# Down projection of row-tile pairs by one-level Strassen, with operand sums in float32r

## The chip, the cores and the metric

The kernel runs on one core of one Trainium2 chip. The metric is the device time of one execution in microseconds (us). "Before" is an already tuned kernel; "the changed kernel" is the same kernel with the change. PE is the matrix engine TensorE (PEld its weight loads), DVE is VectorE, ACT is ScalarE, POOL is GpSimd. PSUM is the memory with eight banks that PE accumulates in, SBUF the working memory.

## The reference, cut to what matters

Part A is a spectral filter with modulation. It is not touched. Part B is a gated feed-forward layer on 2048 rows of 640 values, with 1728 hidden columns, and its result is scaled by `gb` and added to the residual:

```python
def _B_ref(x, w_gate, w_up, w_down):
    g = _silu(x @ w_gate)          # 2048x640 @ 640x1728
    u = x @ w_up
    return g * u @ w_down          # 2048x1728 @ 1728x640
...
h = _layernorm(x, axis=-1) * (1 + cb) + sb
x = x + gb * _B_ref(h, B_w_gate, B_w_up, B_w_down)
```

## The kernel before

The 16 row tiles of 128 rows go through part B in five chunks of 2, 4, 4, 4 and 2 tiles. A chunk first makes the activations `AT` (13 full blocks of 128 hidden columns and one half block, number 13), then does the down projection of its tiles.

```python
chunks = [(0, 2), (2, 4), (6, 4), (10, 4), (14, 2)]
for ci, (t0, n) in enumerate(chunks):
    ...
    AT = (rE if ci % 2 == 0 else rX).cut(0, [NFC, N])
    gu13 = next_banks()[:, 0, 0:N]                       # the half block, gate and up together
    for c5 in range(NC5):
        nc.tensor.matmul(gu13, lhsT=Wp13[:, c5, :], rhs=h2T[:, :, c5, :], ...)      # L822
    ...
    for fc in range(NFC - 1):
        gu = next_banks()
        ...                                              # 5 gate matmuls L836, 5 up matmuls L839
        nc.scalar.activation(sg[:], gu[:, 0, 0:N], ACT.Silu)                        # L842
        nc.vector.tensor_tensor(AT[:, fc, :], gu[:, 1, 0:N], sg[:], ALU.mult)       # L843
        ...
        if ci == 0:      # chunk 0 also scales the down weights by gb, on VectorE
            for f2 in ((13, 0), (1, 2))[fc] if fc < 2 else (fc + 1,) if fc < 12 else ():
                nc.vector.tensor_tensor(Wd_sb[:, f2, :], Wd_sb[:, f2, :], gb_bc[:], ALU.mult)   # L848
            ...          # and normalises chunk 1: ln2_xn is L749, ln2_mod is L764
    for tl in range(n):
        t = t0 + tl
        if tl % 2 == 0:
            pops = [next_banks() for _ in range(2)]
            for h in range(2):
                for s in range(2):                       # half block: 64 rows of the array
                    rows = slice(64 * s, 64 * s + 64)
                    nc.tensor.matmul(pops[s][:, h, 0:320], lhsT=AT[rows, 13, 64 * tl:64 * tl + 128],
                                     rhs=Wd_sb[rows, 13, 320 * h:320 * h + 320], start=True, stop=False)   # L882
        ops4 = pops[tl % 2]
        for lo, hi in ((0, 320), (320, 640)):
            op = ops4[:, lo // 320, 0:320]
            for fc in range(NFC - 1):
                nc.tensor.matmul(op, lhsT=AT[:, fc, tl * 128:(tl + 1) * 128], rhs=Wd_sb[:, fc, lo:hi],
                                 start=False, stop=(fc == NFC - 2))                 # L888
        ...                                              # add the residual x1, store
```

A pair of tiles thus takes 2 x 2 x 13 = 52 full matmuls of 320 columns, and four on half of the array's rows.

Of the kernel before, what the change touches and what calls it, by code (L numbers as in the profile page):

```python
# [9 lines left out]

F32 = mybir.dt.float32
BF16 = mybir.dt.bfloat16
I32 = mybir.dt.int32
ACT = mybir.ActivationFunctionType
ALU = mybir.AluOpType

S, D, FF = 2048, 640, 1728
NT, P = 16, 128
# [3 lines left out]
NFC = 14  # L22
# [106 lines left out]
class _Region:  # L129


    def __init__(self, pool, name, nbytes):
        self.t = pool.tile([P, nbytes // 2], BF16, name=name)

    def cut(self, off, shape, dt=BF16, parts=P):
        n = int(np.prod(shape))
        el = 4 if dt == F32 else 2
        ap = self.t[0:parts, off // 2:off // 2 + n * el // 2]
        if dt == F32:
            ap = ap.bitcast(F32)  # L140
        if len(shape) > 1:
            names = " ".join(f"a{i}" for i in range(len(shape)))
            ap = ap.rearrange(f"p ({names}) -> p {names}", **{f"a{i}": v for i, v in enumerate(shape)})
        return ap
# [8 lines left out]
def adaln_block_kernel(ctx, tc, A_x, A_w_r, A_w_i, B_x, B_w_gate, B_w_up, B_w_down, c, w_mod, out):  # L153
    nc = tc.nc
# [8 lines left out]
    out_v = out.rearrange("o (p t) d -> p (o t) d", t=NT)  # L163
# [2 lines left out]
    const = ctx.enter_context(tc.tile_pool(name="const", bufs=1))  # L166
    big = ctx.enter_context(tc.tile_pool(name="big", bufs=1))

    rX = _Region(big, "rX", 20480)
    rM = _Region(big, "rM", 40960)  # L170
    rA = _Region(big, "rA", 20736)
    rE = _Region(big, "rE", 40960)
    rW = _Region(big, "rW", 49152)
    rH = _Region(big, "rH", 8192 + 2560)
    rL = _Region(big, "rL", 15360 + 4608)


    Ktab = const.tile([P, 576], BF16, name="Ktab")
# [36 lines left out]
    o = 0  # L215
# [6 lines left out]
    oGS = o; o += 768 * 4  # L222
    oSQ = o; o += 256

    SL = rL.cut(15360, [5, 2, 128])

    psum = ctx.enter_context(tc.tile_pool(name="psum", bufs=1, space=bass.MemoryType.PSUM)).tile([P, 8, 512], F32, name="psum")

    def banks(b, n, shape=None, dt=F32):
        ap = psum[:, b:b + n, :].rearrange("p b e -> p (b e)")  # L230
        if dt == BF16:
            ap = ap.bitcast(BF16)
        if shape is not None:
            ap = ap[:, 0:int(np.prod(shape))]
            if len(shape) > 1:
                ap = ap.rearrange("p (a b) -> p a b", a=shape[0])
        return ap
# [87 lines left out]
    if True:  # L325
# [86 lines left out]
        for k in range(NC5):  # L412
# [5 lines left out]
                                op=ALU.add)  # L418
# [73 lines left out]
    if True:  # L492
# [18 lines left out]
        Wd_sb = rA.cut(0, [NFC, D])  # L511
# [65 lines left out]
        def stage_b(g, PP):  # L577
            n = len(groups[g])
            yps = banks(g % 2, 1, [4, 128])
            for ps in (1, 0):  # L580
                for i in range(n):
                    nc.tensor.matmul(yps[:, i, :], lhsT=_rev(PP, 128 * n * ps + i, [[n, 128]]), rhs=identb[:],  # L582
                                     start=(ps == 1 and i == 0), stop=(ps == 0 and i == n - 1))
            Y2 = rL.cut(12288 + 1024 * (g % 4), [4, 128])
            nc.scalar.copy(Y2[:, 0:n, :], yps[:, 0:n, :])  # L585
            return Y2

# [155 lines left out]
    def ln2_pow(t0, n):  # L743
        v = rstd2[:, t0:t0 + n]
        nc.gpsimd.tensor_tensor(v, v, mhalf[:, 0:n], ALU.pow)  # L745
# [5 lines left out]
    def ln2_tr(ci):  # L751
        n = chunks[ci][1]
        nc.sync.dma_start_transpose(
            h2T_all[:, ci % 2, 0:n].rearrange("p tl c q -> p (tl c) q"),
            xn2c[:, 0:n].rearrange("p tl (c q) -> p (tl c) q", c=NC5))
# [48 lines left out]
                ln2_mod(0)  # L804


    oF = 14336
    pair = [1]

    def next_banks():  # L810
        b = banks(2 * pair[0], 2, [2, 512])
        pair[0] = (pair[0] + 1) % 4
        return b

    for ci, (t0, n) in enumerate(chunks):
        N = 128 * n
        h2T = h2T_all[:, ci % 2, 0:n]
        AT = (rE if ci % 2 == 0 else rX).cut(0, [NFC, N])

        gu13 = next_banks()[:, 0, 0:N]  # L820
        for c5 in range(NC5):
            nc.tensor.matmul(gu13, lhsT=Wp13[:, c5, :], rhs=h2T[:, :, c5, :], start=(c5 == 0), stop=(c5 == NC5 - 1))  # L822
        gv = gu13.rearrange("p (j s q) -> p s j q", s=2, q=128)
        f13 = rE.cut(oF, [n // 2, 128], F32)
        m13 = rE.cut(oF + 1024, [n // 2, 128])
        b13 = rE.cut(oF + 1536, [n // 2, 128])
        nc.scalar.activation(m13[0:64], gv[0:64, 1], ACT.Silu)  # L827
        nc.scalar.copy(m13[64:128], gv[64:128, 0])
        nc.scalar.activation(f13[0:64], gv[0:64, 0], ACT.Silu)
        nc.scalar.copy(f13[64:128], gv[64:128, 1])  # L830
        nc.sync.dma_start(b13[0:64], m13[64:128])
        nc.sync.dma_start(b13[64:128], m13[0:64])
        for fc in range(NFC - 1):
            gu = next_banks()
            for c5 in range(NC5):
                nc.tensor.matmul(gu[:, 0, 0:N], lhsT=Wgu[:, 0, c5, fc * 128:(fc + 1) * 128], rhs=h2T[:, :, c5, :],  # L836
                                 start=(c5 == 0), stop=(c5 == NC5 - 1))
            for c5 in range(NC5):
                nc.tensor.matmul(gu[:, 1, 0:N], lhsT=Wgu[:, 1, c5, fc * 128:(fc + 1) * 128], rhs=h2T[:, :, c5, :],  # L839
                                 start=(c5 == 0), stop=(c5 == NC5 - 1))  # L840
            sg = rE.cut(oF + 4096 + 2048 * (fc % 2), [N], F32)
            nc.scalar.activation(sg[:], gu[:, 0, 0:N], ACT.Silu)  # L842
            nc.vector.tensor_tensor(AT[:, fc, :], gu[:, 1, 0:N], sg[:], ALU.mult)  # L843
            if fc == 2:
                nc.vector.tensor_tensor(AT[:, 13, 0:N // 2], f13[:].rearrange("p j q -> p (j q)"), b13[:].rearrange("p j q -> p (j q)"), ALU.mult)
            if ci == 0:
                for f2 in ((13, 0), (1, 2))[fc] if fc < 2 else (fc + 1,) if fc < 12 else ():
                    nc.vector.tensor_tensor(Wd_sb[:, f2, :], Wd_sb[:, f2, :], gb_bc[:], ALU.mult)  # L848
                if fc in (0, 1, 2, 4):
                    i = min(fc, 3)  # L850
                    ln2_act(4 + i // 2, i % 2)
                if fc == 5:
                    ln2_var(2, 4, True)
                    ln2_pow(2, 4)
                if 7 <= fc <= 10:
                    ln2_xn(1, fc - 7)
                if fc == 10:
                    ln2_tr(1)
            elif ci + 1 < len(chunks):
                u0, un = chunks[ci + 1]  # L860
                if 1 <= fc <= un:
                    ln2_bn(u0 + fc - 1, 0)
                    ln2_bn(u0 + fc - 1, 1)
                if fc == un + 1:
                    ln2_var(u0, un, False)
                    ln2_pow(u0, un)
                if un + 2 <= fc < un + 4:
                    for i in range(un // 2 * (fc - un - 2), un // 2 * (fc - un - 1)):
                        ln2_xn(ci + 1, i)
                if fc == un + 3:  # L870
                    ln2_tr(ci + 1)
                if fc == 12:
                    ln2_mod(ci + 1)
        for tl in range(n):
            t = t0 + tl
            xo = rE.cut(oF + 8192 + 1280 * (t % 3), [D])
            if tl % 2 == 0:
                pops = [next_banks() for _ in range(2)]
                for h in range(2):
                    for s in range(2):  # L880
                        rows = slice(64 * s, 64 * s + 64)
                        nc.tensor.matmul(pops[s][:, h, 0:320], lhsT=AT[rows, 13, 64 * tl:64 * tl + 128],  # L882
                                         rhs=Wd_sb[rows, 13, 320 * h:320 * h + 320], start=True, stop=False)
            ops4 = pops[tl % 2]
            for lo, hi in ((0, 320), (320, 640)):
                op = ops4[:, lo // 320, 0:320]
                for fc in range(NFC - 1):
                    nc.tensor.matmul(op, lhsT=AT[:, fc, tl * 128:(tl + 1) * 128], rhs=Wd_sb[:, fc, lo:hi],  # L888
                                     start=False, stop=(fc == NFC - 2))
                if t == NT - 1:  # L890
                    nc.vector.tensor_tensor(xo[:, lo:hi], op, x1[:, t, lo:hi], ALU.add)
                    nc.sync.dma_start(out_v[:, t, lo:hi], xo[:, lo:hi])
            if t < NT - 1:
                nc.vector.tensor_tensor(xo[:].rearrange("p (h m) -> p h m", h=2), ops4[:, :, 0:320],  # L894
                                        x1[:, t, :].rearrange("p (h m) -> p h m", h=2), ALU.add)
                nc.sync.dma_start(out_v[:, t, :], xo[:])
            if ci == 0 and tl == 0:
                ln2_mod(1)


@with_exitstack
# [46 lines left out]
```

## Time and profile before

| | before |
|---|---|
| median of the first runs | 268.01 us (267.82 to 268.99, 3 runs) |
| PE busy | 259.3 of 267.5 us |
| chunk 0, first gate/up matmul to the first of chunk 1 | 86.91 to 109.19, 22.3 us |
| a pair of tiles, start to start | 7.5 us |

The page of the kernel before: the busy times of the engines (us, share, instructions) and the chain of work that ended last, by engine.

```profile
PE 259.3 (97%) x2177; PEld 176.0 (66%) x2177; DVE 150.5 (56%) x363; ACT 110.9 (41%) x207; POOL 47.5 (18%) x101
...
PE 80%; DVE 2%; ACT 2%; issue 1%; ACTq 0%
```

The work of PE on the timeline of before, around chunk 0's down projection and at the start of chunk 1's. Columns: start us, duration us, engine, line, operation, output<-inputs, shapes, number of instructions merged.

```profile
101.74 0.45 PE L882 MATMUL psum<-rA,rE 64*128 64x320 bf16 x4
102.12 7.24 PE L888 MATMUL psum<-rA,rE 128*128 128x320 bf16 x52
109.19 1.24 PE L822 MATMUL psum<-rW,Wp_1277 128*128 128x512 bf16 x5
...
138.43 0.45 PE L882 MATMUL psum<-rA,rX 64*128 64x320 bf16 x4
138.80 7.24 PE L888 MATMUL psum<-rA,rX 128*128 128x320 bf16 x52
145.97 0.45 PE L882 MATMUL psum<-rA,rX 64*128 64x320 bf16 x4
```

Read the starts, not the durations: a matmul's record is longer (0.30 us) than its place in the stream, because they overlap. From 138.80 to 145.97 there are 52 matmuls, 138 ns each on average; most follow the one before after 136 ns. No bracket "[idle before <-releaser]" stands in these lines: PE does not wait. So fewer matmuls should mean less time.

### The profile page before, as it was taken

The page shows a single profiled execution, that of the slowest core. Times are in us where ns is not written, and L with a number is a line of the kernel's source. Part 1 is how long each engine was busy: PE and PEld are TensorE (multiplying, and loading weights), DVE is VectorE, ACT ScalarE, POOL GpSimd, SP SyncE. Part 2 cuts the span into 40 slices and gives each one's busy share as a digit, 9 for nine tenths or more (in the row PEclk, how much of TensorE's full clock was granted, in tenths as well). Part 3 has the DMA queues.
Part 4 walks back from the last instruction along what each step waited for, and adds up shares of the span by engine and source line. Part 5 has one row for each costly group of instructions (what it writes and reads, how often), then busy time and mean ns, then how long its engine had stood idle before and what let it go on. Part 6 is the DMA issues. An engine that isn't in the chain of part 4 may idle for free.

```text
span 267.5 us, 5470 instructions
## 1 busy us (share of the span) xinstructions
PE 259.3 (97%) x2177; PEld 176.0 (66%) x2177; DVE 150.5 (56%) x363; ACT 110.9 (41%) x207; POOL 47.5 (18%) x101
## 2 busy tenths in 40 slices
PE   8999988999999999999999999999999999999995
PEld 3878857999888887544446744445664444768873
DVE  2698689999897795376542148634126533224312
ACT  3678666998778831422230042222023223003310
POOL 4287753686014010001000000100000100000000
PEclk9999999999999999999999999999999999999999
DMA  7989979999978005100610110050110020011001
GB/s 225 394 265 332 343 294 196 218 407 363 288 224 253 9 1 100 59 1 0 70 31 25 51 36 0 0 100 0 49 51 10 0 49 4 25 49 32 1 2 49
DMA packets 42760, 30.79 MB, mean 115 GB/s; under 512 B 21359, under 2 KB 40942, under 8 KB 42350
## 3 DMA queue, kind: packets, MB, share of 16 engines
q1 hardware_dynamic: 42588, 30.23, 39.7%
q8 instruction: 17, 0.28, 0.4%
q10 hardware_dynamic: 146, 0.21, 0.2%
q14 instruction: 9, 0.07, 0.1%
HBM read 22.87 MB, written 4.72 MB: 103 GB/s over the span
## 4 chain that ended last, share of the span: by engine, by line
PE 80%; DVE 2%; ACT 2%; issue 1%; ACTq 0%
PE psum L888 21%; PE psum L839 21%; PE psum L836 21%; PE psum L645 3%; PE psum L582 2%; PE psum L546 2%; PE psum L781 2%; PE psum L822 2%; PE psum L784 1%; PE psum L882 1%; DVE rM L569 1%; PE psum L603 1%; PE psum L634 1%; PE psum L650 1%; ACT rE L618 1%
## 5 line engine op out<-in xcount | busy, mean ns | idle before, releaser
L839 PE MATMUL psum<-rW 128*128 128x512 bf16 (+1 forms) x325 | 66.9, 336 | 0.0
L836 PE MATMUL psum<-rW 128*128 128x512 bf16 (+1 forms) x325 | 66.9, 336 | 0.0
L842 ACT ACTIVATE rE<-psum 128x512 f32<-128x512 f32 (+1 forms) x65 | 33.2, 511 | 68.1 <-PE psum L836 67.9
L839 PEld LDWEIGHTS <-rW 128*128 128x128 bf16 x325 | 31.8, 98 | 24.5
L836 PEld LDWEIGHTS <-rW 128*128 128x128 bf16 x325 | 31.8, 98 | 24.5
L894 DVE TENSOR_TENSOR rE<-psum,rM 128x640 bf16<-128x640 f32 x15 | 12.4, 824 | 41.4 <-PE psum L888 41.4
L843 DVE TENSOR_TENSOR rX<-psum,rE 128x512 bf16<-128x512 f32 x26 | 18.0, 692 | 30.0 <-PE psum L839 23.7
L843 DVE TENSOR_TENSOR rE<-psum,rE 128x256 bf16<-128x256 f32 (+1 forms) x39 | 20.0, 512 | 23.9 <-PE psum L839 18.8
L888 PE MATMUL psum<-rA,rE 128*128 128x320 bf16 x208 | 28.9, 299 | 0.0
L888 PE MATMUL psum<-rA,rX 128*128 128x320 bf16 x208 | 28.9, 299 | 0.0
L745 POOL TENSOR_TENSOR rstd_1285<-rstd_1285,mhalf 128x4 f32<-128x4 f32 (+1 forms) x5 | 4.4, 885 | 129.6 <-DVE rstd_1285 L741 118.0
L888 PEld LDWEIGHTS <-rE 128*128 128x128 bf16 x208 | 20.0, 98 | 8.7 <-issue 1.1
L888 PEld LDWEIGHTS <-rX 128*128 128x128 bf16 x208 | 20.0, 98 | 8.7 <-issue 1.1
L827 ACT ACTIVATE rE<-psum 64x256 bf16<-64x256 f32 (+1 forms) x5 | 1.7, 334 | 49.5 <-PE psum L822 49.5
L569 DVE TENSOR_TENSOR rM<-psum,rW 128x384 bf16<-128x384 f32 (+2 forms) x42 | 20.5, 541 | 1.4 <-PE psum L546 1.1
L385 DVE SCALAR_TENSOR_TENSOR rE<-rE,mv,psum 128x648 bf16<-128x648 f32 (+1 forms) x17 | 14.1, 840 | 2.4 <-PE psum L318 2.1
L786 DVE TENSOR_TENSOR rM<-psum,rX 128x640 f32<-128x640 f32 x16 | 13.0, 818 | 2.8 <-PE psum L784 2.7
L338 ACT COPY rE<-psum 128x640 bf16<-128x640 bf16 x16 | 11.1, 692 | 7.5 <-PE psum L336 7.5
L585 ACT CAST rL<-psum 128x512 bf16<-128x512 f32 (+2 forms) x21 | 12.2, 590 | 3.8 <-PE psum L582 3.7
L582 PE MATMUL psum<-identb,rM 128*128 128x128 bf16 x162 | 12.7, 220 | 0.0
L653 ACT CAST rL<-psum 128x640 bf16<-128x640 f32 x16 | 10.9, 689 | 4.0 <-PE psum L650 3.1
L399 ACT CAST rA<-psum 128x648 bf16<-128x648 f32 x15 | 10.5, 700 | 4.0 <-PE psum L396 3.0
(145 smaller groups left out, 358.0 us busy)
## 6 DMA issues: line engine op xcount, KB each, us to landing
rM<-in_w_mod_dram SPq DMA_DIRECT2D x3, 800.0 KB, 8.8
out_dram<-rE SPq DMA_DIRECT2D x15, 160.0 KB, 1.8
rA<-in_B_w_down_dram SPq DMA_DIRECT2D x1, 2080.0 KB, 17.6
rX<-in_A_x_dram SPq DMA_DIRECT2D x3, 640.0 KB, 9.4
rM<-in_w_mod_dram SPq DMA_DIRECT2D x1, 1600.0 KB, 7.3
rW<-in_B_w_gate_dram SPq DMA_DIRECT2D x2, 640.0 KB, 7.0
rW<-in_B_w_up_dram SPq DMA_DIRECT2D x2, 640.0 KB, 8.2
rW<-in_A_w_i_dram SPq DMA_DIRECT2D x1, 1024.0 KB, 9.7
```

Of the source, the lines that this page charges most:

```text
L338: nc.scalar.copy(hT[:, :, 0:128], _rev(xt, 127, [[128, NC5], [-1, 128]]) if flipped(t) else xt)
L385: nc.vector.scalar_tensor_tensor(Zv[:, h], Cv[:, h], mv[:, t, 0:1], zps[:, h], ALU.mult, ALU.subtract)
L569: nc.vector.tensor_tensor(PP[:, 1:4, hl], xv[:, :, hl], in1, ALU.mult)
L582: nc.tensor.matmul(yps[:, i, :], lhsT=_rev(PP, 128 * n * ps + i, [[n, 128]]), rhs=identb[:], start=(ps == 1 and i == 0), stop=(ps == 0 and ...
L585: nc.scalar.copy(Y2[:, 0:n, :], yps[:, 0:n, :])
L786: nc.vector.tensor_tensor(x1[:, t, :].rearrange("p (m h r) -> p m h r", h=2, r=2), ops[:, :, 0:320].rearrange("p h (r m) -> p m h r", r=2) ...
L836: nc.tensor.matmul(gu[:, 0, 0:N], lhsT=Wgu[:, 0, c5, fc * 128:(fc + 1) * 128], rhs=h2T[:, :, c5, :], start=(c5 == 0), stop=(c5 == NC5 - 1))
L839: nc.tensor.matmul(gu[:, 1, 0:N], lhsT=Wgu[:, 1, c5, fc * 128:(fc + 1) * 128], rhs=h2T[:, :, c5, :], start=(c5 == 0), stop=(c5 == NC5 - 1))
L842: nc.scalar.activation(sg[:], gu[:, 0, 0:N], ACT.Silu)
L843: nc.vector.tensor_tensor(AT[:, fc, :], gu[:, 1, 0:N], sg[:], ALU.mult)
L888: nc.tensor.matmul(op, lhsT=AT[:, fc, tl * 128:(tl + 1) * 128], rhs=Wd_sb[:, fc, lo:hi], start=False, stop=(fc == NFC - 2))
L894: nc.vector.tensor_tensor(xo[:].rearrange("p (h m) -> p h m", h=2), ops4[:, :, 0:320], x1[:, t, :].rearrange("p (h m) -> p h m", h=2), ALU ...
```

## The change

The pair's product is seen as a 2 x 2 block product: two row tiles, 12 of the 13 full hidden blocks in two halves of six (the last, block 12, stays plain), the 640 output columns in two halves of 320. Strassen's scheme (in Winograd's form, with shared partial results) does this with seven half products instead of eight. The intent is to save six of 52 full matmuls in each of seven pairs; chunk 0 stays plain. The price is sums of operands (`S1` to `S4` of activations, `T1` to `T4` of weights, kept in float32r, a 4-byte format, so that the sums lose little), and additions of shared results into the residual. The diff, cut to its core:

```diff
+    T1, T2, T4 = (fE.cut(15360 + 7680 * i, [HK, 320]) for i in range(3))      # fE, fH, fY: float32r; HK = 6
+    T3, B22 = fH.cut(0, [HK, 320]), fY.cut(0, [HK, 320])
...
+    def wd_tables(i):
+        if i == 0:
+            nc.gpsimd.tensor_tensor(T1, B12b, B11, ALU.subtract)
+        elif i == 1:
+            nc.gpsimd.tensor_tensor(T2, B22b, f32(T1), ALU.subtract)
+        elif i == 2:
+            nc.gpsimd.tensor_tensor(T3, B22b, B12b, ALU.subtract)
+            nc.scalar.copy(B22, B22b)
+        else:
+            nc.gpsimd.tensor_tensor(T4, B21, f32(T2), ALU.subtract)
...
+    def down_pair(ATc, t, j, nxt):
+        b0 = [(next_banks(1)) for _ in range(5)]
+        X, Z, Y, W, V = (psum[:, b, 0:320] for b in b0)
...
+        prod(X, lambda k: ATc[:, k, ta:ta + 128], lambda k: B11[:, k], True)      # bf16
+        nc.scalar.copy(cps_[0], X)
+        rest13(Z, 0, 0)                                                           # half-row matmuls
+        rest13(W, 0, 1)
+        prod(Y, sx(0), lambda k: T1[:, k], True)                                  # S1 T1, float32r
+        nxt(0)                                                                    # S1 of the next pair
+        nc.scalar.copy(cps_[1], Y)
+        nc.gpsimd.tensor_tensor(xa[:, 0:320], xa[:, 0:320], cps_[0], ALU.add)
+        prod(X, sx(1), lambda k: T2[:, k], False)                                 # S2 T2 onto X
...
+        prod(Z, lambda k: ATc[:, HK + k, ta:ta + 128], lambda k: B21[:, k], False, False)   # bf16
+        rest12(Z, 0, ta)
...
+        prod(X, sx(2), lambda k: T3[:, k], False)                                 # S3 T3 onto X
...
+        prod(W, lambda k: A22[:, k], lambda k: T4[:, k], False, False)            # float32r
+        rest12(W, 0, tb)
...
+        rest13(Y, 1, 0)
+        rest13(V, 1, 1)
+        rest12(V, 1, tb)
+        prod(Y, sx(3), lambda k: B22[:, k], False, False)                         # float32r
+        rest12(Y, 1, ta)
...
+            if ci and fc in (3, 7, 11):                  # sums of a chunk's first pair, on GpSimd
+                for i in range(5):
+                    a_sum(ATc, 0, i, slice(fc // 2 - 1, fc // 2 + 1), nc.gpsimd)
...
             if ci == 0:
...
                 if fc == 5:
                     ln2_var(2, 4, True)
                     ln2_pow(2, 4)
+                    wd_tables(0)
...
+                if fc == 11:
+                    wd_tables(1)
+                    wd_tables(2)
...
+        if ci == 0:
+            down_plain(ATc, t0, n)
+            wd_tables(3)
+        else:
+            for j in range(n // 2):
+                down_pair(ATc, t0 + 2 * j, j, lambda i: a_sum(ATc, j + 1, i, slice(0, HK), nc.vector) if j + 1 < n // 2 else None)
```

The activations now have one buffer instead of two, and the hidden blocks are made in the order 0, 6, 1, 7, and so on, so that sums can start early.

## The prediction

> What bounds the kernel now. TensorE. The page has PE busy 259.3 of 267.5 us, and the chain that ended last is 80% PE. From 87 us on the timeline of PE has no hole: 52 matmuls of one row-tile pair of the down projection (128x320, bf16) take 7.17 us in the chain, 137.9 ns each; the four half-row ones (64x320) in front add 0.38 us. A pair costs 7.55 us, and the down projection 21.4% of the chain. VectorE is mostly idle there (3.9 to 4.1 us busy in the 15 us of two pairs, by the table of stretches).
>
> What the change does. Seven of the eight pairs (the first stays plain) go from 52+4 to 46+4 matmuls of 320 columns: 12 of 13 full row blocks are done with seven half products instead of eight. 30 of the 46 have float32r operands; the built program has no separate weight load for these, where each bf16 matmul has one.
>
> Saved: 6 x 137.9 ns = 0.83 us a pair, 5.8 us in seven, all on the critical chain, if a float32r matmul of 320 columns keeps the pace of a bf16 one. All hangs on this. For it: the Trainium skill ("FP8 and Floating Point Precision", TensorE Precision Notes) has reduced-precision FP32 read and truncated, and four passes only for true FP32. Against it: "TensorE: Matmul & The Clock Gate", Weight-path perf modes, gives no fast weight load to FP32, and says a weight load takes columns/1.2 ns, so 107 ns for 128 columns (an estimate from that page). Under a 138 ns matmul this hides, if it still runs ahead. If weight loads are exposed, 210 of them at 50 to 107 ns add 10 to 22 us and the kernel is slower.
>
> Added elsewhere (estimates from the trace's durations): VectorE 320-column adds 0.49 us each, six a pair, and four 768-element sums for the second pair of a chunk, about 1 us each: near 7 us in a first pair of 6.7 us, but the second pair has no sums, so it catches up. ScalarE: four 320-column copies (about 0.43 us) and one of 768. GpSimd: three adds a pair, the first pair's sums in thirds during gate/up, four weight tables in chunk 0. ScalarE reads the shared bank X behind about 1 us of other matmuls: enough. S1 of a first pair is needed 3.2 us after the last gate/up block it needs; VectorE plus GpSimd want about 1.5 us. Chunk 0 is doubtful (91 to 102 us): VectorE is 10.4 of 11 us busy, and GpSimd tables now run beside it. I allow 0.3 to 1 us of stalls in all. The tail stays.
>
> Prediction: 268.0 - 5.8 + 0.6 = 262.8; weighing in a slightly worse pace, 263.1 us. Range 261.5 to 274. Faster by over 2%: 0.38; within 2%: 0.42; slower by over 2%: 0.20.
>
> What would show it. Right: a pair takes about 6.7 us in the chain; float32r matmuls come every 138 ns; PE has no holes beyond 0.5 us in the down projection; gate/up groups stay at 1.08 us. Wrong at the pace: float32r matmuls start 160 to 250 ns apart with no wait for another engine. Wrong at the dependencies: PE idle ended by VectorE, GpSimd or ScalarE at the start of products with sums, or by ScalarE at bank X. Wrong at chunk 0: PE idle there.
>
> What would make it wrong: float32r weight loads that do not run ahead, matmuls of more than one pass, or GpSimd sums much slower than its trace durations suggest.

## More of the kernel before

VectorE in chunk 0 of the kernel before. L848 scales a block of down weights, L749 normalises (both read and write SBUF alone), L843 reads one operand from PSUM.

```profile
96.46 0.42 DVE L843 TENSOR_TENSOR rE<-psum,rE 128x256 bf16<-128x256 f32 x1 [0.27 <-PE psum L839]
96.80 0.48 DVE L848 TENSOR_TENSOR rA<-rA,gb_bc 128x640 bf16<-128x640 bf16 x1
97.20 0.61 DVE L749 TENSOR_SCALAR rL<-rM,st_1284,rstd_1285 128x640 bf16<-128x640 f32 x1
```

VectorE is nearly full here, but it keeps up.

## The result, and the profile after

| | before | changed |
|---|---|---|
| median, same rounds | 268.03 us (267.82 to 268.99, 4 runs) | 275.64 us (274.91 to 276.36, 4 runs) |
| ratio | | 1.0276, interval 1.025 to 1.0302: slower |
| chunk 0 | 22.3 us | 85.62 to 116.39, 30.8 us |
| a pair, start to start | 7.50 us | 7.40 us |

The page of the changed kernel: the busy times, the granted PE clock in tenths over 40 slices, and the chain by engine.

```profile
PE 260.1 (95%) x2135; PEld 181.5 (66%) x2135; DVE 183.4 (67%) x402; ACT 130.7 (48%) x251; POOL 117.9 (43%) x174
...
PEclk9999999999999998699999999999999999999999
...
PE 64%; DVE 3%; issue 1%; ACT 0%; DVEq 0%
```

PE has 42 matmuls fewer and is not busy less. Two slices show a lower clock. PEld has as many instructions as PE, so the float32r matmuls do have weight loads in the trace; the prediction's remark on the built program says nothing about their time.

PE in the changed kernel around chunk 0's down projection (L876 half rows, L880 full rows), same columns; the bracket is idle time of PE before the instruction and what ended it.

```profile
99.27 0.71 PE L965 MATMUL psum<-rW 128*128 128x256 bf16 x5
100.22 0.71 PE L968 MATMUL psum<-rW 128*128 128x256 bf16 x5 [0.24 <-DVE fX L972]
100.86 0.31 PE L876 MATMUL psum<-rA,fX 64*128 64x320 bf16 x2
101.47 0.29 PE L876 MATMUL psum<-rA,fX 64*128 64x320 bf16 x1 [0.31 <-DVE fX L972]
102.73 0.29 PE L876 MATMUL psum<-rA,fX 64*128 64x320 bf16 x1 [0.96 <-DVE fX L972]
102.95 1.80 PE L880 MATMUL psum<-rA,fX 128*128 128x320 bf16 x12
108.04 8.51 PE L880 MATMUL psum<-rA,fX 128*128 128x320 bf16 x40 [3.28 <-DVE fX L972]
116.39 1.24 PE L950 MATMUL psum<-rW,Wp_1278 128*128 128x512 bf16 x5
```

Four holes (three brackets of up to 1 us and one of 3.28 us, 4.8 us in all) end with VectorE's L972, the multiplication that makes the last blocks of `AT` (L843 of before). Behind the longest, 40 matmuls take 8.35 us to the next start, where 40 at 136 ns would take 5.4: the clock has dropped. The granted clock in the trace is 1.00 up to 107.18 us, 0.50 from there to 114.00, and 1.00 again: it fell 2.4 us into the hole, which begins at 104.75, and stayed low for 6.8 us. Counted by starts, the waits cost 5.6 us of chunk 0's 8.5, and the slow clock 2.9.

Why is VectorE late? VectorE and then GpSimd in the same stretch (L980 is the weight scaling; L838, L840 and L842 make the tables T1 to T3):

```profile
95.17 0.42 DVE L972 TENSOR_TENSOR fX<-psum,fX 128x256 bf16<-128x256 f32 x1 [0.27 <-PE psum L968]
95.51 3.80 DVE L980 TENSOR_TENSOR rA<-rA,gb_bc 128x640 bf16<-128x640 bf16 x1
...
103.86 3.79 DVE L980 TENSOR_TENSOR rA<-rA,gb_bc 128x640 bf16<-128x640 bf16 x1
107.57 0.41 DVE L972 TENSOR_TENSOR fX<-psum,fX 128x256 bf16<-128x256 f32 x1
```

```profile
95.14 3.82 POOL L838 TENSOR_TENSOR fE<-rA 128x1920 fp32r<-128x1920 bf16 x1
103.22 4.08 POOL L840 TENSOR_TENSOR fE<-rA,fE 128x1920 fp32r<-128x1920 bf16 x1 [4.26 <-DVE rA L980]
107.27 4.06 POOL L842 TENSOR_TENSOR fH<-rA 128x1920 fp32r<-128x1920 bf16 x1
...
```

Two of 14 weight scalings last 3.8 us instead of 0.48, and each ends 0.35 us after a GpSimd table does (99.31 after 98.96, 107.65 after 107.30), so it seems to do most of its work only then. Neither has a semaphore to wait for among its operands in the trace, and the trace counts the time as busy. L972 at 107.57, which reads PSUM and one SBUF operand, runs its usual 0.41 us beside table T3, which began at 107.27.

The Trainium skill, "GPSIMD Engine Reference", section "1. Specifications", has a line on this that the prediction did not use: SBUF interfaces are "Shared with VectorE (contention with DVE instructions in a 2-port perf mode or with two SBUF inputs)". The trace agrees: the two scalings have two inputs in SBUF and stood, L972 has one and did not. It also shows how long they stood: until the GpSimd table was over.

The same trace shows limits of this. In chunk 1, L730 (BATCH_NORM_STATS2, which also works in SBUF alone) took its usual 0.48 us at 127.38, beside a GpSimd sum from 127.14 to 127.81, whereas the normalisation L753 at 136.13 took 0.96 instead of 0.60, beside one that ended at 136.75. The scaling at 94.42 took its usual 0.48 us inside a GpSimd operation on four elements, recorded from 94.17 to 95.18. And the one that starts first can be VectorE: beside an L753 that began at 135.61, the GpSimd sum of 135.78 took 0.97 us instead of 0.67.

The pair. PE in chunk 1's first pair (L894 the products, L899 half rows, L903 block 12):

```profile
145.53 0.98 PE L894 MATMUL psum<-rA,fX 128*128 128x320 bf16 x6
146.44 0.31 PE L899 MATMUL psum<-rA,fX 64*128 64x320 bf16 x2
146.68 2.03 PE L894 MATMUL psum<-fE 128*128 128x320 f32 x12
148.54 0.99 PE L894 MATMUL psum<-rA,fX 128*128 128x320 bf16 x6
...
149.40 1.15 PE L894 MATMUL psum<-fH,fE 128*128 128x320 f32 x6
...
152.93 0.57 PE L894 MATMUL psum<-rA,fX 128*128 128x320 bf16 x3
```

From 145.53 to 152.93, 7.40 us, and no bracket: PE waits for no engine. The single starts in the trace give the reason. A float32r matmul follows the one before after 147 ns, a bf16 one after 136. And where half-row matmuls meet full-row ones, about 0.1 us is lost going in and 0.1 to 0.2 us coming out. Before, the four half-row matmuls stood together and this was paid once a pair (232 and 228 ns instead of 136 at the two edges, 0.19 us); the changed kernel pays it twice (0.3 us at the first place, where the next matmul is float32r, and 0.2 at the second).

The account of the difference: chunk 0 costs 30.77 - 22.28 = 8.5 us more, seven pairs save about 0.1 us each, and the four gate/up stages that follow are 0.09 us shorter each. That makes +7.4 us; the medians differ by 7.6. (The profiled runs differ only by 6.1 us, because the untouched part ahead of the feed-forward layer took 86.91 us in one and 85.62 in the other; it is seen between 85.5 and 87.0 in the experiments too.) That the sum comes so near is partly luck: the 8.5 us hold 6.8 us at half clock, and the other three timed runs of the changed kernel had a mean granted clock of 0.993 instead of 0.988, which fits about half as much.

### The profile page after: what moved, and what is told of

The parts are those of the page before. It is cut to its first block, busy times and chain, and to the rows that moved or that the text cites. A ratio compares the mean times of both kernels' runs of the same rounds, so it can differ in the third digit from the quotient of the medians.

```text
span 273.6 us, 5643 instructions
## 1 busy us (share of the span) xinstructions
PE 260.1 (95%) x2135; PEld 181.5 (66%) x2135; DVE 183.4 (67%) x402; ACT 130.7 (48%) x251; POOL 117.9 (43%) x174
## 4 chain that ended last, share of the span: by engine, by line
PE 64%; DVE 3%; issue 1%; ACT 0%; DVEq 0%
PE psum L968 20%; PE psum L965 20%; PE psum L894 16%; PE psum L880 3%; DVE rA L980 2%; PE psum L903 2%; PE psum L950 2%; PE psum L899 1%; DVE fX L972 1%; DVE rL L753 1%; ACT rL L657 0%; DVE rW L866 0%; PE psum L785 0%; PE psum L788 0%; DVEq L972 0%
## 5 line engine op out<-in xcount | busy, mean ns | idle before, releaser
L972 DVE TENSOR_TENSOR fX<-psum,fX 128x512 bf16<-128x512 f32 (+1 forms) x65 | 37.9, 583 | 52.9 <-PE psum L968 39.1
L971 ACT ACTIVATE fX<-psum 128x512 f32<-128x512 f32 (+1 forms) x65 | 33.2, 511 | 52.5 <-PE psum L965 48.2
L852 POOL TENSOR_TENSOR fE<-fX 128x256 fp32r<-128x256 bf16 x12 | 8.6, 720 | 79.6 <-DVE fX L972 57.6
L894 PE MATMUL psum<-fE 128*128 128x320 f32 x126 | 21.5, 314 | 0.0
L894 PEld LDWEIGHTS psum<-fE 128*128 128x128 f32 x126 | 18.8, 188 | 1.0
L866 DVE TENSOR_TENSOR rA<-psum,rM 128x320 bf16<-128x320 f32 (+1 forms) x20 | 10.0, 516 | 8.6 <-PE psum L880 4.7
L860 ACT CAST fE<-fX 128x256 fp32r<-128x256 bf16 (+1 forms) x15 | 7.4, 490 | 15.2 <-DVE fX L972 13.6
L589 ACT CAST rY<-psum 128x512 bf16<-128x512 f32 (+2 forms) x21 | 12.2, 589 | 3.8 <-PE psum L586 3.7
L894 PE MATMUL psum<-rA,fX 128*128 128x320 bf16 x84 | 13.8, 300 | 0.0
L880 PE MATMUL psum<-rA,fX 128*128 128x320 bf16 x52 | 10.3, 373 | 3.3 <-DVE fX L972 3.3
L980 DVE TENSOR_TENSOR rA<-rA,gb_bc 128x640 bf16<-128x640 bf16 x14 | 13.2, 953 | 0.0
```

What stands on the lines that cost most here:

```text
L589: nc.scalar.copy(Y2[:, 0:n, :], yps[:, 0:n, :])
L880: nc.tensor.matmul(pops[tl % 2][:, h, 0:320], lhsT=ATc[:, fc, tl * 128:(tl + 1) * 128], rhs=Wd_sb[:, fc, 320 * h:320 * h + 320], start=Fal ...
L894: nc.tensor.matmul(o, lhsT=lhs(k), rhs=rhs(k), start=(start and k == 0), stop=(stop and k == HK - 1), skip_group_check=True)
L972: nc.vector.tensor_tensor(ATc[:, ff, :], gu[:, 1, 0:N], sg[:], ALU.mult)
```

## The experiments

Theory P: VectorE operations that use SBUF on both sides stand still while a long GpSimd operation runs; PE then runs dry in chunk 0, and its clock falls. Rivals: D, that VectorE waits for GpSimd through a data dependency on the weights; F, that the pace of float32r matmuls is the loss. For the pair, the theory has two parts: the pace of float32r (weights or streaming), and the second switch to half rows. Eleven kernels were run, in three groups, each group on one chip with its own runs of before (medians 269.19, 267.96 and 269.03 us).

### tables_only: the tables are made and not used

```diff
-            if ci and fc in (3, 7, 11):
-                for i in range(5):
-                    a_sum(ATc, 0, i, slice(fc // 2 - 1, fc // 2 + 1), nc.gpsimd)
...
-            for j in range(n // 2):
-                down_pair(ATc, t0 + 2 * j, j, lambda i: ...)
+            down_plain(ATc, t0, n)
```

> All chunks use the plain down projection; the four weight tables are still made on GpSimd at the same places but never read. Theory P (the loss is chunk 0: VectorE's two-input operations stop while a two-input GpSimd operation runs, and the TensorE clock falls in the hole that follows): chunk 0 from its first gate/up matmul to the first of chunk 1 stays near 31 us instead of 22.5, and the time is about 268.0 + 8.5 = 276.5 us. Theory F (the loss is the pace of float32r matmuls): no float32r matmul is left, so about 268 to 269 us.

Measured: 276.62 us (275.99 to 277.34), ratio 1.0278 (1.0254 to 1.0302), result correct. There is no float32r matmul in it, and it is as slow as the changed kernel. F falls as the main cause: the loss is that of making the tables, or of the new buffers, which this kernel shares (vec_only, below, rules these out). The hole is there again:

```profile
108.12 7.28 PE L880 MATMUL psum<-rA,fX 128*128 128x320 bf16 x40 [3.28 <-DVE fX L972]
```

Here the granted clock was 0.50 from 108.67 to 112.08, 3.4 us instead of 6.8, and the 40 matmuls took 7.3 us to the next start (115.42).

### tables_copied: one input instead of two

```diff
-            nc.gpsimd.tensor_tensor(T1, B12b, B11, ALU.subtract)
+            nc.gpsimd.tensor_copy(T1, B12b)
```

and likewise for T2, T3 and T4.

> Wrong result on purpose: each GpSimd table is a one-input copy of the same 1920 elements in place of a two-input subtraction, reading the same rows of the scaled down weights. Theory P (second SBUF input of GpSimd holds the port VectorE needs): no weight-scaling operation over 0.6 us, no PE hole before chunk 0's down projection, chunk 0 22.5 us, time about 267 us. Rival D (VectorE waits for GpSimd through a dependency on the down weights or tables, whatever the GpSimd operation) or GpSimd simply writing much: two scaling operations remain as long as the GpSimd copies, and the time stays above 271 us.

Measured: 268.77 us (268.48 to 269.94), ratio 0.9994 (0.997 to 1.0018); the result is wrong. The expectation "no weight scaling over 0.6 us" failed. VectorE and then GpSimd:

```profile
95.56 1.75 DVE L980 TENSOR_TENSOR rA<-rA,gb_bc 128x640 bf16<-128x640 bf16 x1
...
101.85 1.74 DVE L980 TENSOR_TENSOR rA<-rA,gb_bc 128x640 bf16<-128x640 bf16 x1
```

```profile
95.17 1.78 POOL L838 CAST fE<-rA 128x1920 fp32r<-128x1920 bf16 x1
101.14 2.11 POOL L840 CAST fE<-rA 128x1920 fp32r<-128x1920 bf16 x1 [4.18 <-DVE rA L980]
```

A one-input GpSimd operation holds VectorE too, as long as it lasts: the two scalings end at 97.31 and 103.59, again 0.35 us after the copies (96.95 and 103.25). So the second input of GpSimd is not what does it; it only makes the operation twice as long. P was right about the stall and wrong about its condition, and D was still open, because the copies read the same weights.

### unrelated: GpSimd works in scratch

The plain kernel of tables_only again, with all tables replaced by three operations on memory that VectorE never touches:

```diff
-            nc.gpsimd.tensor_tensor(T1, B12b, B11, ALU.subtract)
+            nc.gpsimd.memset(f32(T1), 0.0)
+            nc.gpsimd.tensor_copy(f32(T2), f32(T1))
+            nc.gpsimd.tensor_tensor(f32(T4), f32(T1), f32(T2), ALU.subtract)
```

> All chunks plain; in place of the first weight table GpSimd does, one after the other, a memset, a one-input copy and a two-input subtraction of 1920 float32 elements, all in scratch that VectorE never touches; no other table. Theory P (an operation of GpSimd holds something that VectorE's operations with two SBUF inputs or doubled rate need, whatever the data): weight-scaling and normalising operations of VectorE in that stretch are as long as the GpSimd operation beside them, about 4 us at the subtraction and 1.8 to 2 us at the copy; the memset, which reads nothing, may or may not do it. Theory D (dependency through the down weights): all weight-scaling operations 0.48 us, no PE hole, chunk 0 22.5 us.

Measured, one look: 276.44 us, result correct. GpSimd, then VectorE (L972 is the weight scaling here, L967 the multiplication that reads PSUM):

```profile
95.84 1.70 POOL L838 MEMSET fE<- 128x1920 f32 x1
97.60 1.92 POOL L839 COPY fE<-fE 128x1920 f32<-128x1920 f32 x1
99.60 4.35 POOL L840 TENSOR_TENSOR fE<-fE 128x1920 f32<-128x1920 f32 x1
```

```profile
96.23 0.48 DVE L972 TENSOR_TENSOR rA<-rA,gb_bc 128x640 bf16<-128x640 bf16 x1
96.63 1.25 DVE L753 TENSOR_SCALAR rL<-rM,st,rstd 128x640 bf16<-128x640 f32 x1
97.80 0.40 DVE L967 TENSOR_TENSOR fX<-psum,fX 128x256 bf16<-128x256 f32 x1
98.13 1.73 DVE L972 TENSOR_TENSOR rA<-rA,gb_bc 128x640 bf16<-128x640 bf16 x1
99.78 4.51 DVE L753 TENSOR_SCALAR rL<-rM,st,rstd 128x640 bf16<-128x640 f32 x1
```

D falls: no data is shared and VectorE still stands, and the three long operations end 0.34 us after the memset, the copy and the subtraction. L967, with its PSUM operand, passes beside the copy in 0.40 us. Beside the memset, which reads nothing, the two-input L972 passes in 0.48 us while the TENSOR_SCALAR does not (1.25 instead of 0.60). That is one look at one instruction each; these runs do not show why the memset stops the one and not the other.

### filled: PE kept busy in the hole

```diff
                 for fc in range(NFC - 1):
+                    if tl == 0 and h == 0 and fc == 12:
+                        for _ in range(14):
+                            nc.tensor.matmul(banks(2, 1, [512]), lhsT=ones[:], rhs=..., start=True, stop=True)
```

> Changed kernel plus 14 unused 512-column matmuls (3.0 us) in the PE hole before the last row block of chunk 0's first tile. If the clock fell because PE idled 3.3 us, the 40 matmuls behind it take about 5.5 us instead of 8.5 and the time falls by about 3 us, to 272.6 us. If the clock falls for another reason, the time stays at 275 to 276 us.

Measured: 274.4 us (273.92 to 275.97), ratio 1.0215 (1.0185 to 1.0244): 0.6% better than the changed kernel's 1.0276, about 1.6 us, not 3. PE:

```profile
108.00 5.61 PE L884 MATMUL psum<-rA,fX 128*128 128x320 bf16 x40 [0.27 <-DVE fX L976]
113.45 0.59 PE L954 MATMUL psum<-rW,Wp 128*128 128x512 bf16 x2
115.35 0.81 PE L954 MATMUL psum<-rW,Wp 128*128 128x512 bf16 x3 [1.30 <-DVE rW L768]
```

The 40 matmuls take 5.45 us to the next start instead of 8.35: the lower clock was a consequence of the idle time. The Trainium skill, "TensorE: Matmul & The Clock Gate", "Part 1: The HAM clock gate", puts the fall to half the clock after an idle window of about 3.4 us. The traces agree in that the clock fell at a hole of 3.28 us, not at one of 1.2 us (tables_copied, 1.000), and stayed low for 3.41 us (tables_only) or 6.82 (the changed kernel). But the length of the hole does not fix the moment: with the same hole the clock fell 2.4 us into it in the changed kernel, and 0.55 us after its end in tables_only. The missing gain has two reasons. Most timed runs of the changed kernel had less than 3 us to lose, going by their granted clock (above). And in this trace the gain was in part given back at once: PE arrived sooner at chunk 1 and found `ln2_mod` (L768, whose three operations on VectorE took 4.76 us instead of 1.05) held up beside table T4.

### tables_late: tables in small pieces, written later in the program

```diff
+    def wd_piece(m):
+        i, k = divmod(m, HK)
+        if i == 0:
+            nc.gpsimd.tensor_tensor(T1[:, k], B12b[:, k], B11[:, k], ALU.subtract)
...
+            if ci == 1 and fc < 12:
+                wd_piece(2 * fc)
+                wd_piece(2 * fc + 1)
```

> Tables made in chunk 1's gate/up phase, in 24 pieces of 320 columns (about 0.65 us each), instead of four pieces of 1920 in chunk 0. Correct result. Theory P: chunk 0 returns to 22.5 us, the longest VectorE wait is one piece (about 0.7 us), PE has no hole in chunk 1, and what is left is 7 pairs of 7.40 instead of 7.55 us: 268.0 - 1.0 = 267.0 us (266.5 to 267.5). If the port blocks VectorE enough in chunk 1 to stop PE, holes appear there and the time is 268 to 271 us.

Measured: 270.33 us (269.93 to 271.43), ratio 1.0053 (1.0031 to 1.0075), result correct. Missed: the time lies in the second range, but the waits of 0.77 and 0.42 us are in chunk 0; in chunk 1 there is one of 0.29. GpSimd:

```profile
95.03 5.78 POOL L839 TENSOR_TENSOR fE<-rA 128x320 fp32r<-128x320 bf16 x6
```

The pieces stand in chunk 1's part of the program and ran in chunk 0. GpSimd had nothing else to do and the weights were ready, so it ran ahead. Weight scalings now last 0.75 us instead of 0.48, and chunk 0 takes 24.7 us (85.50 to 110.19). Smaller pieces make each stall shorter and leave the sum of GpSimd's time beside VectorE, here even longer (5.78 us for T1 against 3.82 in one piece).

### columns: what sets the pace of float32r

```diff
-        prod(X, sx(1), lambda k: T2[:, k], False)
+        prod(X, sx(1), lambda k: T2[:, k], False, c=128)
-        prod(X, sx(2), lambda k: T3[:, k], False)
+        prod(X, sx(2), lambda k: T3[:, k], False, c=192)
-        prod(W, lambda k: A22[:, k], lambda k: T4[:, k], False, False)
+        prod(W, lambda k: A22[:, k], lambda k: T4[:, k], False, False, c=256)
```

> Wrong result on purpose: the float32r products S2 T2, S3 T3 and A22 T4 stream 128, 192 and 256 columns, S1 T1 and S4 B22 320. If float32r weight loads set the pace: start to start 147 ns at 320 columns and no lower than about 107 to 147 ns for the others (a floor). If each float32r matmul streams its columns at the full rate and pays a fixed 13 ns on top: 147, 120, 93 and 67 ns for 320, 256, 192 and 128 columns.

Measured, one look (result wrong, as meant), medians of the start-to-start times within a product (`c` limits the columns; the bf16 figures at 192 and 128 columns are from part A):

| columns | float32r | bf16 in the same traces |
|---|---|---|
| 320 | 145 to 147 ns | 136 ns |
| 256 | 118 ns | 109 ns |
| 192 | 112 ns | 82 ns |
| 128 | 111 ns | 56 ns |

Both theories hold in part. At 192 and 128 columns float32r has a floor of 111 ns, which bf16 has not, and at 256 and 320 a float32r matmul costs 9 to 11 ns more than a bf16 one of the same width. The floor is near what the Trainium skill says of weight loads ("TensorE: Matmul & The Clock Gate", section "LDWEIGHTS (loading the stationary operand)": columns over 1.2, so an estimate of 107 ns for 128); that the weight loads make it is not shown. At the 320 columns of this kernel the floor does not bind: the weight loads, 188 ns long in the trace against 98 for bf16, run ahead. What the extra 11 ns at 320 columns is made of these runs do not tell.

### sums_bf16: the same products with bf16 operands

```diff
-    fE = _Region(big, "fE", 40960, "E", F32R)
+    fE = _Region(big, "fE", 40960, "E")
```

and likewise for `fH` and `fY`.

> Sums, tables and the two copies in bf16 instead of float32r; nothing else changes, chunk 0 keeps its stall (up to what bf16 output saves). Correct if the tolerance allows. If the pace of float32r costs 10.7 ns x 30 matmuls and about 0.1 us after the half-row matmuls, a pair takes 6.9 to 7.0 us instead of 7.40 and the time falls by about 3 us, to 272 to 273 us. If the pair's extra time lies elsewhere (half-row matmuls alone, PSUM banks), it stays above 7.3 us.

Measured: 271.67 us (271.02 to 272.34), ratio 1.0124 (1.0089 to 1.016), result correct. Two pairs take 13.89 us, 6.95 us each, instead of 7.40, within the range expected. The time fell a little more than the pairs account for (0.45 x 7 = 3.2 us; the ratios differ by 1.5%, 4.1 us); chunk 0 was 1.1 us shorter in this profile, in which the clock was low for 3.4 us instead of 6.8.

### halves_once: the half-row matmuls together

```diff
-        rest13(Z, 0, 0)
-        rest13(W, 0, 1)
         prod(Y, sx(0), lambda k: T1[:, k], True)
...
+        rest13(Z, 0, 0, True)
+        rest13(W, 0, 1, True)
         rest13(Y, 1, 0)
         rest13(V, 1, 1)
```

> The four half-row matmuls of a pair stand together, as in the kernel before, instead of two and two. If each switch from full-row to half-row matmuls and back costs about 0.2 to 0.3 us because the next weight load does not run ahead, a pair takes about 7.1 us instead of 7.40, and the time falls by about 2 us, to 273.5 us. If the switch costs nothing, a pair stays at 7.40.

Measured: 273.69 us (273.53 to 273.86), ratio 1.0203 (1.0179 to 1.0227), result correct. Two pairs take 14.20 us, 7.10 each. The second switch cost 0.30 us a pair, as much as read from the starts.

### vec_only, vec_once, vec_once_bf16_direct: putting it right, one step at a time

vec_only makes the tables on VectorE, in halves, in chunk 1, where it has time; GpSimd keeps out of chunk 0.

```diff
+        i, h = divmod(i, 2)
+        ks = slice(3 * h, 3 * h + 3)
         if i == 0:
-            nc.gpsimd.tensor_tensor(T1, B12b, B11, ALU.subtract)
+            nc.vector.tensor_tensor(T1[:, ks], B12b[:, ks], B11[:, ks], ALU.subtract)
...
+            if ci == 1:
+                for i in {0: (0,), 4: (1,), 5: (2,), 8: (3,), 9: (4, 5), 10: (6,), 11: (7,)}.get(fc, ()):
+                    wd_tables(i)
```

> Changed kernel with the weight tables made by VectorE itself, in eight half tables spread over chunk 1's gate/up phase; GpSimd does nothing in chunk 0. float32r and the order of matmuls as in the changed kernel. If the GpSimd tables are the whole of chunk 0's loss, chunk 0 and its down projection take 22.3 us again, PE has no hole, and the seven pairs at 7.40 instead of 7.50 us leave 268.0 - 0.7 = 267.3 us (266.8 to 267.8). If something else in the new layout costs chunk 0 time (single activation buffer, shared memory with the residual), it stays over 24 us.

Measured: 267.53 us (266.98 to 268.66), ratio 0.9962 (0.9939 to 0.9986). PE in chunk 0's down projection, to be held against the same lines of before and of the changed kernel:

```profile
100.53 0.45 PE L878 MATMUL psum<-rA,fX 64*128 64x320 bf16 x4
100.90 7.24 PE L882 MATMUL psum<-rA,fX 128*128 128x320 bf16 x52
107.98 1.24 PE L952 MATMUL psum<-rW,Wp 128*128 128x512 bf16 x5
```

Chunk 0 takes 22.3 us (85.69 to 107.98) as before the change, without a hole. The whole loss there was the GpSimd tables beside VectorE; the single activation buffer costs nothing.

vec_once is vec_only with the change of halves_once.

> As vec_only, with the four half-row matmuls of a pair together. Pairs take 7.10 us: 268.0 - 7 x 0.40 = 265.2 us (264.6 to 266). Result right, precision as in the changed kernel.

Measured: 266.29 us (265.24 to 266.59), ratio 0.9901 (0.988 to 0.9921), result correct. This is just above the expected range, which was reckoned from 268.0; before took 269.03 in these rounds.

vec_once_bf16_direct has the bf16 sums as well, and reads A22 and B22 where they lie instead of copying them.

```diff
-        else:
-            nc.scalar.copy(A22[:, ks], a22)
...
-        prod(W, lambda k: A22[:, k], lambda k: T4[:, k], False, False)
+        prod(W, lambda k: ATc[:, HK + k, tb:tb + 128], lambda k: T4[:, k], True, False)
...
-        prod(Y, sx(3), lambda k: B22[:, k], False, False)
+        prod(Y, sx(3), lambda k: B22b[:, k], False, False)
```

> As vec_once, with sums and tables in bf16 and without the two copies that float32r needed (A22 and B22 are read where they lie). Every matmul at 136 ns, one switch to half rows a pair: 48 slots x 0.136 + 0.2 = 6.73 us a pair, 268.0 - 7 x 0.77 = 262.6 us (262 to 263.5), about 2% faster than the kernel before, with a correct result as for bf16 sums before. If VectorE or PSUM banks become the limit in the pairs, holes of PE appear in the down projection and the time is 264 us or more.

Measured: 262.86 us (262.78 to 264.48), ratio 0.9791 (0.9765 to 0.9816), result correct. This is faster than both kernels, by 2.1% than the kernel before; the verdict at the 2% mark is "unclear", because the interval crosses it. The busy line of its page, and the beginning, the half-row matmuls and the end of its first pair:

```profile
PE 252.4 (97%) x2135; PEld 170.5 (65%) x2135; DVE 174.1 (67%) x410; ACT 122.5 (47%) x235; POOL 98.7 (38%) x170
```

```profile
137.48 0.98 PE L893 MATMUL psum<-rA,fX 128*128 128x320 bf16 x6
...
142.73 0.45 PE L898 MATMUL psum<-rA,fX 64*128 64x320 bf16 x4
...
144.21 0.98 PE L893 MATMUL psum<-rA,fX 128*128 128x320 bf16 x6
```

From 137.48 to 144.21 is 6.73 us a pair, the expected sum of 48 places of 136 ns (46 full matmuls and two places for the four half-row ones) and one switch of 0.19. PE busy fell by 6.9 us against before.

The three steps and what each brought, from the means of the same rounds: keeping GpSimd out of chunk 0 takes the ratio from 1.0276 to 0.9962 (the first was measured against other runs of before), one switch less brings 0.6%, bf16 operands without copies 1.1%.

## Why the prediction was wrong, point by point

1. "TensorE bounds the kernel": right. Fewer places in the PE stream gave less time as soon as nothing else stood in the way.
2. "All hangs on this", the pace of float32r: wrong. The decisive step was the one mentioned last, "Chunk 0 is doubtful (91 to 102 us): VectorE is 10.4 of 11 us busy, and GpSimd tables now run beside it. I allow 0.3 to 1 us of stalls in all." It named the right place, and "PE idle there" as the sign of it, but mis-sized it: chunk 0 took 8.5 us longer in the profiled run, 5.6 by waits and 2.9 by the clock. Tables_only shows it without any Strassen product; vec_only shows it gone.
3. Its mechanism had not been understood. The prediction gives no mechanism for the stalls; the nearest it names is GpSimd sums slower than their durations. The runs showed the reverse: GpSimd went on and VectorE's scalings stood until it was done, 3.8 us at a time, which unrelated data showed to be no dependency. With hindsight, the estimate should have been two to four tables of 4 us against an engine with 0.6 us of slack. The skill's line on shared interfaces was there to be read.
4. The clock: not foreseen. A recorded hole of 3.3 us in PE led to half the clock during part of the 40 matmuls behind it, 2.9 us more in the profiled run and 1.9 in that of tables_only; filled shows that the hole was the cause.
5. "Saved: 6 x 137.9 ns = 0.83 us a pair": the gain measured 0.10 us. Of the rest, the pace of float32r takes 30 x 11 ns = 0.33 us, and the second switch to half rows 0.30. The prediction had counted half-row matmuls as 0.38 us in all, wherever they stand; their cost lies in the edges. Sums_bf16, columns and halves_once show the two terms. They leave 0.20 of the 0.83 us; the remaining 0.1 us is not assigned.
6. Float32r weight loads "at 50 to 107 ns" exposed: did not happen at 320 columns, except behind half-row matmuls. The 160 to 250 ns named as the sign of a wrong pace was not reached either; it was 147. Nor were there "matmuls of more than one pass": 147 ns against 136 agrees with what the prediction took from the precision notes. (The formula for weight loads that the prediction took from the skill stands in the section on LDWEIGHTS, not in the one it named.)
7. VectorE's 7 us in a first pair, the ScalarE reads of the shared bank and the sums of a first pair on GpSimd: right. PE has no hole in any pair of the changed kernel.
8. "Gate/up groups stay at 1.08 us": right in chunks 1 to 3 (29.14 us for 135 matmuls, 29.23 before).
9. The range of 261.5 to 274 did not hold the 275.64 us. With chunk 0 put right but float32r and both switches kept, the changed kernel would have been at 0.9962, "within 2%"; the 262.8 of the sum is met by the kernel with bf16 sums and one switch, at 262.86. That the digits agree is luck: before took 269.03 in those rounds, not 268.0.

## What to carry to other kernels

An idle engine is not free work: here a long GpSimd operation stopped VectorE's weight scalings and normalisations in SBUF until it was over, while operations with a PSUM operand, and L730, passed. So before moving a long GpSimd operation next to a VectorE that is nearly full, count its duration as a stop of such operations, and remember that an engine with nothing to wait for runs its part long before the place where it stands in the program. When counting matmuls saved, count places in the PE stream from start to start, with the edges between full-row and half-row work and the data type's own pace, and look for the place where PE could run dry for as long as here (3.2 to 3.3 us; a hole of 1.2 left the clock alone), since the clock then added a loss of its own.

## What the Trainium skill lacked or had wrong

- Not lacking, though missed here: "GPSIMD Engine Reference", section 1, does not say how long VectorE stands (to the end of the GpSimd operation: 3.80 us for a scaling of 0.48, 1.75 beside a one-input copy, 4.51 for a normalisation of 0.60) or what a memset does (0.48 us for the scaling, 1.25 for the normalisation, one look each). "SBUF — State Buffer", section "Who interferes with whom", treats both, and these numbers agree with it. What neither has is the scaling that took its usual 0.48 us inside the recorded 1.01 us of a GpSimd operation on four elements.
- "TensorE: Matmul & The Clock Gate" has no pace for float32r. Here: 147 ns at 320 columns (bf16 136), 118 at 256 (bf16 109), and a floor of 111 ns at 128 columns (bf16 56).
- The same page, Part 3, says when weight loads overlap with running matmuls in row tiles, and no page says how long a change between full-row and half-row matmuls takes: 0.19 us for going in and out between bf16 matmuls, 0.30 us with a float32r matmul behind.
- The same page does not say how much work an idle window may hold. Six traces have a fall in chunk 0 (the changed kernel, tables_only, unrelated, columns, sums_bf16, halves_once). Counting 3.41 us back from each fall, that stretch held 0.2 to 1.0 us of PE records, and the one before it, with 2.0 us or more, had not lowered the clock. After the fall, a stretch with 2.2 or 2.6 us of work (unrelated and the changed kernel) did not bring the clock back; a full one did.
